# A delta-rule layer with a gated MoE layer behind it: which engine issues which DMA, and what the scheduler reckons

## The chip, the cores and the metric

The kernel runs on one core of a Trainium2 chip. Five engines of a core run their own instruction streams in order: TensorE (PE, with its weight loads as PEld), VectorE (DVE), ScalarE (ACT), GpSimd (POOL) and SyncE (SP), which here only issues DMAs. The metric is the device time in microseconds of one execution; the median of three runs of the kernel before is 515.21 us (514.75 to 515.44).

## The reference

Two layers follow each other. The first is a delta rule over 768 tokens, for 4 batches of 8 heads of 48 dimensions:

```python
k_n = k / (np.linalg.norm(k, axis=-1, keepdims=True) + 1e-06)
for t in range(S):
    kt, vt, bt = (k_n[:, :, t], v[:, :, t], beta[:, :, t, None])
    y[:, :, t] = np.einsum('bhd,bhde->bhe', q[:, :, t], state)
    v_old = np.einsum('bhde,bhd->bhe', state, kt)
    state = state + bt[:, :, :, None] * np.einsum('bhd,bhe->bhde', kt, vt - v_old)
```

Its output, as 3072 rows of 384, goes through an MLP with a softmax gate and a layer norm:

```python
h = x @ w_in                                    # 384 -> 1024
e = np.exp(h - np.max(h, axis=-1, keepdims=True))
solu = h * (e / (np.sum(e, axis=-1, keepdims=True) + 1e-09))
mu, var = np.mean(solu, -1), np.var(solu, -1)   # per row
out = ((solu - mu) / np.sqrt(var + 1e-06) * g_ln) @ w_out
```

## The kernel before, in words

The 768 tokens are cut into 12 chunks of 64. A unit is one chunk of two of the four batches, so there are 24 units of 128 rows (two batches of 64 tokens on the partitions), named chunk_half: 6_1 is chunk 6, second pair. Within a chunk the recurrence becomes matrix algebra with the inverse of a triangular matrix, and these inverses are made for several units at once: group m = 0 holds the two units of chunk 0, groups 1 to 5 four units each, group 6 the two units of chunk 11. (The prediction calls such a group a batch.)

A unit and its group pass these stages:

- **load and gram** (`load_kq`, `load_kv`, `gram`): keys and queries are loaded (tile kq; kv holds keys and values). TensorE forms k k^T and k q^T in PSUM; ScalarE copies the first to g, VectorE masks the second into pm. Two DMAs a unit store g into the DRAM tile gd (line 526).
- **inversion of a group** (`to_inv`, `norms`, `inv_begin`, `inv_step`, `inv_end`): gd is loaded back in another order as ginv (four or eight DMAs), VectorE makes norms and scales it to y, and GpSimd eliminates in 30 steps of two instructions (tiles itmp and y). `inv_end` copies y transposed on ScalarE, stores both to DRAM (zd, xd) and loads them in ten smaller DMAs in matmul order as zt, gx and gy. These DMAs that change an order are called relayouts; each moves runs of 128 bytes.
- **tlevel**: TensorE joins the 32-wide blocks into 64-wide inverses (mps, ScalarE's msb and zt).
- **chain**, the recurrence: kps and yps from the state, r = v - kps on VectorE, ups = inverse times r, ScalarE's copy u, then cps and yps, and the state's sum. The output is split into two fp16 parts xh (ScalarE) and xl (VectorE), which two DMA transposes turn into xth and xtl (`sp.transpose`, line 703).
- **moe_h**: 18 matmuls into h, then max, exponential e, product pr, the fp16 parts ph (ScalarE) and pl (VectorE), two DMA transposes to pth and ptl (line 745), a second pass e over pr, and statistics.
- **moe_out**: 24 matmuls into ops, oc on VectorE and ScalarE, and one DMA that stores the result (line 772).

All of it is not emitted as it is written. Every call is recorded as an operation with an engine, an occupancy and a latency in ns, and a priority that counts in units; `Recorder.order` (line 178) then plays the engines forward, and gives each engine, when it is free, the ready operation of the lowest priority number. It also follows which tiles of each ring are free. What it decides is emitted as a fixed order on each engine; on the chip an engine executes that order and waits where something is late. The occupancies come from `Engine` (a base and so much an element) and `Queue` (5 ns a KB, landing 2000 ns later). All 385 DMAs here stand on `sp`, SyncE's queue; a second `Queue` on ScalarE, `aq`, is made but not used. Each DMA signals one of eight semaphores in turn, so it also waits until the DMA eight before it, whichever queue that is on, has landed.

Of the kernel before, what the change touches and what calls it, by code (L numbers as in the profile page):

```python
# [16 lines left out]
P = 128  # L17
# [93 lines left out]


class Op:
    __slots__ = ("eng", "occ", "lat", "calls", "prio", "seq", "preds", "left", "succs", "avail", "start", "end", "roots", "slack")


class Recorder:
# [13 lines left out]

        return Pool()

    def add(self, eng, fn, args, kw, occ, lat, slack=0):
        views = [("out" if i == 0 else "in", a) for i, a in enumerate(args)]
        views += [("out" if k in ("out", "accum_out") else "in", a) for k, a in kw.items()]
        views = [(k, a) for k, a in views if isinstance(a, View)]
        if self.group is not None and self.group.calls and self.group.eng == eng:
            op = self.group
        else:  # L140
            op = Op()
            op.eng, op.occ, op.lat, op.calls, op.prio, op.seq = eng, 0.0, 0.0, [], self.prio, len(self.ops)
            op.preds, op.slack = {}, slack
# [34 lines left out]
    def order(self, free):  # L178
# [19 lines left out]
        while True:  # L198
            best = None
            for name, (t, fut, ready) in engs.items():  # L200
                if ready:
                    s = t
                elif fut:
                    s = max(t, fut[0][0])
                else:
                    continue
                if best is None or s < best[0]:
                    best = (s, name)
            if best is None:
                break  # L210
            t, name = best
            e = engs[name]
            while e[1] and e[1][0][0] <= t:
                o = heapq.heappop(e[1])[2]
                heapq.heappush(e[2], (o.prio, o.seq, o))
            o = heapq.heappop(e[2])[2]
            new = [r for r in o.roots if r.ring is not None and r.tile is None]
            wait = None
            for r in new:
                n = sum(x.ring is r.ring for x in new)  # L220
                f = sorted(r.ring.free)
                if len(f) < n:
                    wait = r.ring.waiting
                elif f[n - 1] > t and wait is None:
                    wait = f[n - 1]
            if isinstance(wait, list):
                wait.append(o)
                continue
            if wait is not None:
                heapq.heappush(e[1], (wait, o.seq, o))  # L230
                continue
            for r in new:
                r.tile = 0
                r.ring.free.remove(max(x for x in r.ring.free if x <= t))
            o.start = t
            e[0] = t + o.occ
            o.end = t + o.lat
            done.append(o)
            for r in o.roots:
                r.left -= 1  # L240
                r.free_at = max(r.free_at, t + o.occ if r.engs == {"DVE"} or r.engs == {"POOL"} else o.end)
                if not r.left and r.ring is not None:
                    r.ring.free.append(r.free_at)
                    for w in r.ring.waiting:
                        heapq.heappush(engs[w.eng][1], (max(w.avail, r.free_at), w.seq, w))
                    r.ring.waiting.clear()
            for s in o.succs:
                s.avail = max(s.avail, o.end if s.eng != name or name == "SP" else t + o.occ)
                s.left -= 1
                if not s.left:  # L250
                    s.avail += s.slack
                    heapq.heappush(engs[s.eng][1], (s.avail, s.seq, s))
# [15 lines left out]
class Engine:  # L268


    def __init__(self, rec, name, real, base, per, lat):
        self.rec, self.name, self.engine, self.base, self.per, self.lat = rec, name, real, base, per, lat

    def __getattr__(self, op):
        fn = getattr(self.engine, op)

        def call(*args, n=None, ns=None, slack=0, **kw):
            if ns is None:
                if n is None:
                    v = kw["in_"] if op == "tensor_reduce" else kw["out"] if "out" in kw else args[0]  # L280
                    n = v.count()
                ns = self.base + self.per * n + (190 if "accum_out" in kw else 0)
            return self.rec.add(self.name, fn, args, kw, ns, self.lat, slack)

        return call

# [1 line left out]
class Queue:  # L288


    def __init__(self, rec, name, real):
        self.rec, self.name, self.engine = rec, name, real

    def dma_start(self, kb, **kw):
        return self.rec.add(self.name, self.engine.dma_start, (), kw, kb * 5.0, 2000)

    def transpose(self, kb, **kw):
        return self.rec.add(self.name, self.engine.dma_start_transpose, (), kw, kb * 5.0, 2000)


def chunks_of(m):
# [4 lines left out]
def kernel(  # L306
# [23 lines left out]
    ps_ch, ps_y, ps_f, ps_h, ps_m = (pool(f"ps_{t}", n, **ps) for t, n in (("ch", 2), ("y", 1), ("f", 2), ("h", 1), ("m", 1)))  # L330

    real = nc
    pe = Engine(rec, "PE", nc.tensor, 0, 0, 200)
    dve = Engine(rec, "DVE", nc.vector, 150, 1.04, 80)
    act = Engine(rec, "ACT", nc.scalar, 110, 0.96, 100)
    gps = Engine(rec, "POOL", nc.gpsimd, 200, 1.8, 100)
    sp = Queue(rec, "SP", nc.sync)
    aq = Queue(rec, "ACT", nc.scalar)

    def half(b2):  # L340
        return slice(C * b2, C * b2 + C)
# [35 lines left out]
    def to_f32(u, raw, scale, n, nm):  # L377
# [10 lines left out]
        dve.tensor_scalar(out=u, in0=hi, scalar1=3, scalar2=0x3FFFFFF8, op0=ALU.logical_shift_left, op1=ALU.bitwise_and)  # L388
        dve.scalar_tensor_tensor(out=u, in0=lo, scalar=29, in1=u, op0=ALU.logical_shift_right, op1=ALU.bitwise_or)
        dve.scalar_tensor_tensor(out=u, in0=hi, scalar=-(1 << 30), in1=u, op0=ALU.bitwise_and, op1=ALU.bitwise_or)  # L390
        gps.tensor_tensor(out=f, in0=f, in1=c, op=ALU.mult)

    def load_w_in(k, q, t0, t1):
# [104 lines left out]
    def gram(m, u, t0):  # L498
# [30 lines left out]
    ginv, yt = {}, {}  # L529
# [31 lines left out]
    def inv_step(m, j):  # L561
# [3 lines left out]
        for eng, c0, c1 in parts:  # L565
            if c1 <= c0:
                continue
            c = c1 - c0
            tmp = p1.tile([P, 256], F32, tag=f"itmp{eng.name}", name=f"itmp_{m}_{j}_{c0}")
            tv = tmp[:, 0 : c * n].rearrange("p (c i) -> p c i", i=n)  # L570
            eng.tensor_tensor(
                out=tv, in0=y[:, c0:c1, j : j + 1].to_broadcast([P, c, n]),
                in1=b[:, j : j + 1, j + 1 : 32].to_broadcast([P, c, n]), op=ALU.mult,
            )
            eng.tensor_tensor(out=y[:, c0:c1, j + 1 : 32], in0=y[:, c0:c1, j + 1 : 32], in1=tv, op=ALU.add)

    def inv_end(m):
        y, x1 = yt[m], ginv[m]
# [12 lines left out]
        for b in range(4):  # L591
            blk = b % 2
            r0 = 32 * b
            rows = slice(r0, r0 + 32)
            sp.dma_start(kb=128, out=zz[rows, 0:n, blk * 32 : blk * 32 + 32], in_=zd[r0 : r0 + n].rearrange("l j i -> j l i"))
            if blk == 0:
                for t, r1 in ((xx, r0), (xy, r0 + 32)):
                    sp.dma_start(kb=128, out=t[r1 : r1 + 32, 0:n], in_=xd[r0 : r0 + n].rearrange("l j i -> j l i"))
            else:
                sp.dma_start(kb=128, out=xx[rows, 0:n], in_=src[rows, 0:n, 0:32])  # L600
        ztx[m], gxt[m] = zz, (xx, xy)


# [45 lines left out]
    def chain(m, u, tb, tu, tk):  # L649
# [59 lines left out]
    def moe_h(ch, bp, t0):  # L709
# [31 lines left out]
        dve.scalar_tensor_tensor(out=pl, in0=pr, scalar=sc, in1=ph, op0=ALU.mult, op1=ALU.subtract)  # L741
# [17 lines left out]
    def moe_out(ch, bp, t0):  # L759
# [169 lines left out]
```

## Time and profile before

| what | value |
|---|---|
| median of 3 runs | 515.21 us (514.75 to 515.44) |
| the profiled execution's own time | 512.04 us |
| its span, first to last instruction | 510.2 us |
| busy PE, DVE, POOL, ACT | 72%, 62%, 58%, 38% of the span |
| mean granted TensorE clock | 0.920 |
| DMA queue q1, share of 16 engines | 70.8%, 180560 packets, 71.06 MB |

The page gives each engine's busy time, the chain that ended last, and groups of instructions with the idle time before them and what ended it. Almost every row has line 265, the helper's line that emits; so instructions are told apart by their tiles (zt<-zd is a load of zt from zd). SPq is SyncE's queue: its rows are the time that one issue took, not the transfer. The first 100 us prepare the weights and the first two groups; from then on units follow each other.

### The profile page before, as it was taken

To read this page: it belongs to the slowest core of one execution; us is meant where nothing else is said; L and a number is where in the kernel's file an instruction comes from. 1 tells how busy PE (TensorE), PEld (TensorE's weight loads), DVE (VectorE), ACT (ScalarE), POOL (GpSimd) and SP (SyncE) were. 2 spreads that over 40 slices of the span, in tenths; PEclk is the share of its full clock that TensorE was granted. 3 is DMA by queue.
4 is the path that set the end of the run, shared out by engine and by line. 5 is a ranking of instruction groups with operands and counts; after the bars stand their busy time and mean duration, and the time that the engine had idled before them with its cause. 6 is when DMAs were issued, how large, how long until landed. Compare 5 with 4: busy or idle time off the path is not lost.

```text
span 510.2 us, 18246 instructions
## 1 busy us (share of the span) xinstructions
PE 368.2 (72%) x7744; PEld 233.9 (46%) x7744; DVE 318.6 (62%) x791; ACT 192.9 (38%) x382; POOL 294.0 (58%) x506
## 2 busy tenths in 40 slices
PE   3510070689579488997598997787969797899974
PEld 3410070455346345665366564444635464566532
DVE  3599999887884383655088664256597355455670
ACT  2210241465522143536144544224345345454450
POOL 3378385966558998984016886008989898100000
PEclk9999999877876699998799998898989899999998
DMA  8685662987989949977999587985656866744332
GB/s 212 159 255 98 155 169 65 161 171 174 172 162 165 179 113 160 168 135 161 189 165 144 145 162 151 160 162 95 107 118 144 145 114 128 131 64 99 73 68 61
DMA packets 180640, 72.21 MB, mean 142 GB/s; under 512 B 165520, under 2 KB 168976, under 8 KB 180560
## 3 DMA queue, kind: packets, MB, share of 16 engines
q1 hardware_dynamic: 180560, 71.06, 70.8%
q8 instruction: 60, 0.98, 0.9%
q14 instruction: 20, 0.16, 0.1%
HBM read 37.21 MB, written 16.52 MB: 105 GB/s over the span
## 4 chain that ended last, share of the span: by engine, by line
POOL 28%; PE 22%; DVE 19%; issue 10%; DMA 9%; SPq 7%; ACT 4%; POOLq 0%; DVEq 0%; ACTq 0%
POOL y L265 13%; POOL itmp L265 11%; PE h L265 7%; SPq L265 7%; PE ops L265 7%; DVE y L265 5%; DVE itmp L265 4%; DMA zt<-zd 3%; DMA ginv<-gd 3%; PE mps L265 2%; DVE wf L265 2%; DVE rst L265 1%; DVE st L265 1%; PE kps L265 1%; PE yps L265 1%
## 5 line engine op out<-in xcount | busy, mean ns | idle before, releaser
L265 POOL TENSOR_TENSOR y<-y,itmp 128x84 f32<-128x84 f32 (+16 forms) x190 | 100.7, 530 | 14.6
L265 POOL TENSOR_TENSOR itmp<-y,ginv 128x84 f32<-128x84 f32 (+16 forms) x190 | 93.3, 491 | 14.0
L265 DVE TENSOR_REDUCE st<-h 128x1 f32<-128x1024 f32 x24 | 29.3, 1222 | 87.5 <-PE h L265 82.2
L265 PE MATMUL qk<-kq 48*64 48x64 f32 x768 | 40.4, 269 | 24.9 <-DVE pm L265 15.6
L265 PE MATMUL gram<-kq 48*64 48x64 f32 x768 | 43.2, 270 | 18.8 <-DMA kq<-kq_dram 11.5
L265 POOL TENSOR_TENSOR st<-st,nhalf 128x1 f32<-128x1 f32 x24 | 13.2, 551 | 64.1 <-DVE st L265 64.1
L265 PEld LDWEIGHTS gram<-kq 48*64 48x64 f32 x768 | 37.5, 178 | 25.7 <-ACT g L265 6.3
L265 PEld LDWEIGHTS <-pth 128*128 128x128 f16 x384 | 37.6, 99 | 25.5 <-issue 1.7
L265 PE MATMUL h<-win_hi,xtl 128*128 128x512 f16 x144 | 45.4, 419 | 5.3 <-DVE pr L265 2.6
L265 PE MATMUL mps<-zt,gx 32*32 32x32 f32 x768 | 13.5, 205 | 48.6 <-issue 28.9
L265 PE MATMUL h<-win_lo,xth 128*128 128x512 f16 x144 | 46.7, 421 | 1.7 <-POOL win_lo L265 1.7
L265 PEld LDWEIGHTS qk<-kq 48*64 48x64 f32 x768 | 35.8, 178 | 25.3 <-DVE pm L265 16.1
L265 PEld LDWEIGHTS <-xth 128*128 128x128 f16 x288 | 28.4, 105 | 39.7 <-issue 14.8
L265 PE MATMUL ops<-wout_hi,ptl 128*128 128x384 f16 x192 | 38.7, 345 | 8.7 <-DMA ptl<-pl 6.8
L265 PE MATMUL h<-win_hi,xth 128*128 128x512 f16 x144 | 43.4, 411 | 0.0
L265 ACT ACTIVATE e<-h,st 128x1024 f32<-128x1024 f32 x24 | 26.7, 1114 | 38.0 <-DVE st L265 26.4
L265 POOL TENSOR_SCALAR_AFFINE_SELECT y<-y 128x1024 f32<-128x1024 f32 x7 | 9.4, 1346 | 53.5 <-DVE y L265 53.5
L265 DVE TENSOR_SCALAR st<-st 128x1 f32<-128x1 f32 (+1 forms) x216 | 35.5, 165 | 5.6
L265 PE MATMUL ops<-wout_lo,pth 128*128 128x384 f16 x192 | 36.9, 334 | 0.0
L265 PEld LDWEIGHTS mps<-zt,gx 32*32 32x32 f32 x768 | 10.1, 117 | 56.9 <-issue 34.8
L265 PE MATMUL ops<-wout_hi,pth 128*128 128x384 f16 x192 | 35.5, 326 | 0.0
L265 PE MATMUL cps<-u,kv 64*64 64x48 f32 x704 | 28.9, 235 | 9.1 <-ACT u L265 3.2
(94 smaller groups left out, 860.4 us busy)
## 6 DMA issues: line engine op xcount, KB each, us to landing
kq<-kq_dram SPq DMA_DIRECT2D x48, 192.0 KB, 4.5
kv<-kv_dram SPq DMA_DIRECT2D x24, 384.0 KB, 4.3
gd<-g SPq DMA_DIRECT2D x48, 128.0 KB, 3.3
out_dram<-oc SPq DMA_DIRECT2D x24, 192.0 KB, 2.2
zd<-y SPq DMA_DIRECT2D x7, 512.0 KB, 2.6
wi<-w_in_dram SPq DMA_DIRECT2D x6, 512.0 KB, 4.4
wo<-w_out_dram SPq DMA_DIRECT2D x8, 384.0 KB, 4.0
ginv<-gd SPq DMA_DIRECT2D x20, 128.0 KB, 4.2
```

Source lines behind the costliest of these rows:

```text
L265: fn(*[real(a) for a in args], **{k: real(a) for k, a in kw.items()})
```

## The change

Three kinds of edit. **Issue:** the transposes (xth, xtl, pth, ptl), the stores of g and the stores of the result go to `aq`, ScalarE's queue; loads and relayouts stay on SyncE. **Reckoning:** a DMA on ScalarE occupies it for 400 ns in the scheduler; on SyncE it counts its KB, at least 500 ns, or 1.2 ns a run; a landing is 2300 ns later; TensorE's times are multiplied by 1.06; some VectorE operations get times of their own; the 190 ns for an accumulated output are dropped. **Holding:** `rec.hold(pm)` lets the plan take pm's buffer when the gram matmuls start.

```diff
             for s in o.succs:
-                s.avail = max(s.avail, o.end if s.eng != name or name == "SP" else t + o.occ)
+                s.avail = max(s.avail, o.end if s.eng != name or o.queued else t + o.occ)
...
-                ns = self.base + self.per * n + (190 if "accum_out" in kw else 0)
-            return self.rec.add(self.name, fn, args, kw, ns, self.lat, slack)
+                ns = self.base + self.per * n
+            return self.rec.add(self.name, fn, args, kw, ns * self.scale, self.lat, slack)
...
-    def dma_start(self, kb, **kw):
-        return self.rec.add(self.name, self.engine.dma_start, (), kw, kb * 5.0, 2000)
+    def __init__(self, rec, name, real, issue=None):
+        self.rec, self.name, self.engine, self.issue = rec, name, real, issue
+
+    def add(self, fn, kw, ns):
+        occ = ns if self.issue is None else self.issue
+        return self.rec.add(self.name, fn, (), kw, occ, 2300 + ns - occ, queued=True)
+
+    def dma_start(self, kb, runs=0, **kw):
+        return self.add(self.engine.dma_start, kw, max(500.0, kb * 5.0, runs * 1.2))
 
     def transpose(self, kb, **kw):
-        return self.rec.add(self.name, self.engine.dma_start_transpose, (), kw, kb * 5.0, 2000)
+        return self.add(self.engine.dma_start_transpose, kw, kb * 5.0)
...
-    pe = Engine(rec, "PE", nc.tensor, 0, 0, 200)
+    pe = Engine(rec, "PE", nc.tensor, 0, 0, 200, 1.06)
...
-    aq = Queue(rec, "ACT", nc.scalar)
+    aq = Queue(rec, "ACT", nc.scalar, 400)
...
+            rec.hold(pm)
...
-            sp.dma_start(kb=128, out=gdt[m][half(b2), u], in_=g[half(1 - b2)])
+            aq.dma_start(kb=128, out=gdt[m][half(b2), u], in_=g[half(1 - b2)])
...
-                    kb=128, out=gi[32 * b + 16 * z : 32 * b + 16 * z + n],
+                    kb=128, runs=32 * n, out=gi[32 * b + 16 * z : 32 * b + 16 * z + n],
...
-            sp.transpose(kb=96, out=t, in_=x)
+            aq.transpose(kb=96, out=t, in_=x)
...
-            sp.transpose(kb=256, out=t, in_=x)
+            aq.transpose(kb=256, out=t, in_=x)
...
-        sp.dma_start(kb=192, out=out[ch, bp], in_=t)
+        aq.dma_start(kb=192, out=out[ch, bp], in_=t)
```

The diff does not show what the scheduler makes of it. In the rows below a number behind a tile's name is a buffer's; zd_3, xd_3, zt_1 and gx_3 belong to group 3, and a pair such as 4_0 is a unit.

SyncE's queue around group 3's relayouts, before:

```order
L265 DMA xd_3_3316<-ginv_3_2308 32x1024 x2
L265 DMA zt_1_278<-zd_3_3296 32x32x32 x3
L265 DMA gx_3_2399<-xd_3_3316 32x32x32
L265 DMA gy_3_3421<-xd_3_3316 32x32x32
L265 DMA_TRANSPOSE xth_4_0_3431<-xh_4_0_3417 128x3x128
L265 DMA gx_3_2399<-xd_3_3316 32x32x32
L265 DMA gd_4_2357<-g_8_0_3436 64x512 x2
L265 DMA_TRANSPOSE pth_3_0_3464<-ph_3_0_3444 128x8x128
L265 DMA_TRANSPOSE xtl_4_0_3476<-xl_4_0_3459 128x3x128
L265 DMA_TRANSPOSE ptl_3_0_3491<-pl_3_0_3467 128x8x128
L265 DMA gy_3_3421<-xd_3_3316 32x32x32
L265 DMA zt_1_278<-zd_3_3296 32x32x32
```

and now:

```order
L265 DMA xd_3_3312<-ginv_3_2288 32x1024 x2
L265 DMA kq_9_0_3319<-kq_dram 48x1024 x2
L265 DMA zt_1_272<-zd_3_3286 32x32x32
L265 DMA gx_3_2472<-xd_3_3312 32x32x32
L265 DMA gy_3_3432<-xd_3_3312 32x32x32
L265 DMA zt_1_272<-zd_3_3286 32x32x32 x2
L265 DMA gx_3_2472<-xd_3_3312 32x32x32
L265 DMA gy_3_3432<-xd_3_3312 32x32x32
L265 DMA zt_1_272<-zd_3_3286 32x32x32
```

The four transposes and the two stores of g that stood between the relayouts are gone from this queue; a prefetch of kq stands ahead.

SyncE's queue between group 4's last relayout and the loads of ginv for group 5, before:

```order
L265 DMA zt_0_188<-zd_4_4686 32x32x32
L265 DMA gd_5_4100<-g_10_1_4730 64x512 x2
L265 DMA_TRANSPOSE xth_6_1_4853<-xh_6_1_4843 128x3x128
L265 DMA kq_11_1_4858<-kq_dram 48x1024 x2
L265 DMA_TRANSPOSE pth_5_1_4932<-ph_5_1_4862 128x8x128
L265 DMA_TRANSPOSE ptl_5_1_4956<-pl_5_1_4894 128x8x128
L265 DMA_TRANSPOSE xtl_6_1_4971<-xl_6_1_4885 128x3x128
L265 DMA out_0_dram<-oc_5_0_4936 128x384
L265 DMA ginv_5_5011<-gd_5_4100 32x32x32 x4
```

and now:

```order
L265 DMA gx_4_3721<-xd_4_4637 32x32x32
L265 DMA gy_4_4741<-xd_4_4637 32x32x32
L265 DMA zt_0_189<-zd_4_4609 32x32x32
L265 DMA ginv_5_4826<-gd_5_4135 32x32x32 x4
L265 DMA kq_11_1_4918<-kq_dram 48x1024 x2
```

The loads of ginv follow the relayouts directly; kq comes behind them.

ScalarE between the exponential of unit 5_1 and the copy u of unit 7_0, before:

```order
L265 ACTIVATE ph_5_1_4862<-pr_5_1_4845,st_5_1_4818 128x1024
L265 ACTIVATE msb_4_0_4892<-mps0_4_0_4866 128x128
L265 ACTIVATE e_5_1_4826,st_5_1_4818<-pr_5_1_4845,st_5_1_4818 128x1024
L265 ACTIVATE oc_5_0_4936<-oc_5_0_4936,st_5_0_4492 128x384
L265 COPY zt_0_188<-mps0_4_0_4866 32x4x32 x2
L265 COPY zt_0_188<-mps32_4_0_4940 32x4x32 x2
L265 ACTIVATE msb_4_1_5009<-mps0_4_1_4974 128x128
L265 COPY u_7_0_5014<-ups_7_0_4992 128x384
```

and now, from the transpose of xh on:

```order
L265 DMA_TRANSPOSE xth_6_1_4851<-xh_6_1_4844 128x3x128
L265 ACTIVATE ph_5_1_4875<-pr_5_1_4847,st_5_1_4822 128x1024
L265 ACTIVATE msb_4_0_4890<-mps0_4_0_4856 128x128
L265 DMA_TRANSPOSE pth_5_1_4895<-ph_5_1_4875 128x8x128
L265 ACTIVATE e_5_1_4829,st_5_1_4822<-pr_5_1_4847,st_5_1_4822 128x1024
L265 DMA_TRANSPOSE ptl_5_1_4957<-pl_5_1_4892 128x8x128
L265 DMA_TRANSPOSE xtl_6_1_4960<-xl_6_1_4883 128x3x128
L265 COPY zt_0_189<-mps0_4_0_4856 32x4x32 x2
L265 COPY zt_0_189<-mps32_4_0_4900 32x4x32 x2
L265 ACTIVATE oc_5_0_4955<-oc_5_0_4955,st_5_0_4501 128x384
L265 DMA out_0_dram<-oc_5_0_4955 128x384
L265 ACTIVATE msb_4_1_5019<-mps0_4_1_4978 128x128
```

ScalarE's own work keeps its order nearly; four transposes and a store now stand between its instructions. The copy u of unit 7_0 is the next row.

More of the change, by code (lines that the diff above doesn't have):

```diff
@@ L113 @@
 class Op:
-    __slots__ = ("eng", "occ", "lat", "calls", "prio", "seq", "preds", "left", "succs", "avail", "start", "end", "roots", "slack")
+    __slots__ = ("eng", "occ", "lat", "calls", "prio", "seq", "preds", "left", "succs", "avail", "start", "end", "roots", "slack", "queued")
 class Recorder:
@@ L132, in pool, with add @@
         return Pool()
-    def add(self, eng, fn, args, kw, occ, lat, slack=0):
+    def add(self, eng, fn, args, kw, occ, lat, slack=0, queued=False):
         views = [("out" if i == 0 else "in", a) for i, a in enumerate(args)]
@@ L142, in add @@
             op.eng, op.occ, op.lat, op.calls, op.prio, op.seq = eng, 0.0, 0.0, [], self.prio, len(self.ops)
-            op.preds, op.slack = {}, slack
+            op.preds, op.slack, op.queued = {}, slack, queued
             self.ops.append(op)
@@ L268, with __init__ @@
 class Engine:
-    def __init__(self, rec, name, real, base, per, lat):
-        self.rec, self.name, self.engine, self.base, self.per, self.lat = rec, name, real, base, per, lat
+    def __init__(self, rec, name, real, base, per, lat, scale=1.0):
+        self.rec, self.name, self.engine, self.base, self.per, self.lat, self.scale = rec, name, real, base, per, lat, scale
     def __getattr__(self, op):
@@ L281, in call @@
                     n = v.count()
-                ns = self.base + self.per * n + (190 if "accum_out" in kw else 0)
-            return self.rec.add(self.name, fn, args, kw, ns, self.lat, slack)
+                ns = self.base + self.per * n
+            return self.rec.add(self.name, fn, args, kw, ns * self.scale, self.lat, slack)
         return call
 class Queue:
-    def __init__(self, rec, name, real):
-        self.rec, self.name, self.engine = rec, name, real
-    def dma_start(self, kb, **kw):
-        return self.rec.add(self.name, self.engine.dma_start, (), kw, kb * 5.0, 2000)
+    def __init__(self, rec, name, real, issue=None):
[5 more added lines that the diff above has]
+        return self.add(self.engine.dma_start, kw, max(500.0, kb * 5.0, runs * 1.2))
     def transpose(self, kb, **kw):
-        return self.rec.add(self.name, self.engine.dma_start_transpose, (), kw, kb * 5.0, 2000)
+        return self.add(self.engine.dma_start_transpose, kw, kb * 5.0)
 def chunks_of(m):
@@ L387, in to_f32 @@
         u = u.bitcast(I32)
-        dve.tensor_scalar(out=u, in0=hi, scalar1=3, scalar2=0x3FFFFFF8, op0=ALU.logical_shift_left, op1=ALU.bitwise_and)
-        dve.scalar_tensor_tensor(out=u, in0=lo, scalar=29, in1=u, op0=ALU.logical_shift_right, op1=ALU.bitwise_or)
-        dve.scalar_tensor_tensor(out=u, in0=hi, scalar=-(1 << 30), in1=u, op0=ALU.bitwise_and, op1=ALU.bitwise_or)
+        dve.tensor_scalar(ns=250 + 1.3 * n, out=u, in0=hi, scalar1=3, scalar2=0x3FFFFFF8, op0=ALU.logical_shift_left, op1=ALU.bitwise_and)
+        dve.scalar_tensor_tensor(ns=250 + 1.3 * n, out=u, in0=lo, scalar=29, in1=u, op0=ALU.logical_shift_right, op1=ALU.bitwise_or)
+        dve.scalar_tensor_tensor(ns=250 + 1.3 * n, out=u, in0=hi, scalar=-(1 << 30), in1=u, op0=ALU.bitwise_and, op1=ALU.bitwise_or)
         gps.tensor_tensor(out=f, in0=f, in1=c, op=ALU.mult)
@@ L570, in inv_step @@
             tv = tmp[:, 0 : c * n].rearrange("p (c i) -> p c i", i=n)
+            ns = 230 + 1.04 * c * n if eng is dve else None
             eng.tensor_tensor(
-                out=tv, in0=y[:, c0:c1, j : j + 1].to_broadcast([P, c, n]),
+                ns=ns, out=tv, in0=y[:, c0:c1, j : j + 1].to_broadcast([P, c, n]),
                 in1=b[:, j : j + 1, j + 1 : 32].to_broadcast([P, c, n]), op=ALU.mult,
             )
-            eng.tensor_tensor(out=y[:, c0:c1, j + 1 : 32], in0=y[:, c0:c1, j + 1 : 32], in1=tv, op=ALU.add)
+            eng.tensor_tensor(ns=ns, out=y[:, c0:c1, j + 1 : 32], in0=y[:, c0:c1, j + 1 : 32], in1=tv, op=ALU.add)
     def inv_end(m):
@@ L594, in inv_end @@
             rows = slice(r0, r0 + 32)
-            sp.dma_start(kb=128, out=zz[rows, 0:n, blk * 32 : blk * 32 + 32], in_=zd[r0 : r0 + n].rearrange("l j i -> j l i"))
+            sp.dma_start(kb=128, runs=1024, out=zz[rows, 0:n, blk * 32 : blk * 32 + 32], in_=zd[r0 : r0 + n].rearrange("l j i -> j l i"))
             if blk == 0:
                 for t, r1 in ((xx, r0), (xy, r0 + 32)):
-                    sp.dma_start(kb=128, out=t[r1 : r1 + 32, 0:n], in_=xd[r0 : r0 + n].rearrange("l j i -> j l i"))
+                    sp.dma_start(kb=128, runs=1024, out=t[r1 : r1 + 32, 0:n], in_=xd[r0 : r0 + n].rearrange("l j i -> j l i"))
             else:
-                sp.dma_start(kb=128, out=xx[rows, 0:n], in_=src[rows, 0:n, 0:32])
+                sp.dma_start(kb=128, runs=1024, out=xx[rows, 0:n], in_=src[rows, 0:n, 0:32])
         ztx[m], gxt[m] = zz, (xx, xy)
@@ L740, in moe_h @@
         act.activation(ph, pr, AF.Copy, scale=sc)
-        dve.scalar_tensor_tensor(out=pl, in0=pr, scalar=sc, in1=ph, op0=ALU.mult, op1=ALU.subtract)
+        dve.scalar_tensor_tensor(ns=1420, out=pl, in0=pr, scalar=sc, in1=ph, op0=ALU.mult, op1=ALU.subtract)
         pts = []
```

## The prediction

> **What bounds the kernel now.** I read the page first, then the busy time by stage, then what TensorE and SyncE wait for, then SyncE's queue around those waits.
>
> ```profile
> PE 368.2 (72%) x7744; PEld 233.9 (46%) x7744; DVE 318.6 (62%) x791; ACT 192.9 (38%) x382; POOL 294.0 (58%) x506
> POOL 28%; PE 22%; DVE 19%; issue 10%; DMA 9%; SPq 7%; ACT 4%; POOLq 0%; DVEq 0%; ACTq 0%
> ```
>
> No engine is full over the whole span, and the chain that ended last changes engine all the time; SyncE's queue (SPq) and transfers (DMA) hold 16% of it. So the stages have to be taken apart. The columns of the next view are busy us of PE, PEld, DVE, ACT and POOL, then the granted clock, the busy share of the DMA engines and GB/s.
>
> ```profile
> 100.00:205.00 105.00, 80.48 (x1744) 50.35 (x1743) 70.34 (x157) 40.27 (x84) 79.76 (x117) 0.78 0.88 161
> 205.00:485.00 280.00, 241.95 (x5093) 149.98 (x5091) 159.59 (x415) 122.52 (x246) 151.25 (x274) 0.95 0.71 135
> ```
>
> From 205 us on TensorE works 241.95 of 280 us. That stage is TensorE's, with 280 - 241.95 = 38.05 us of gaps, and only what closes or opens such gaps can move the end. The gaps that a transfer ends are these (the wait is in brackets, first the group's total in 205 to 485 us):
>
> ```profile
> PE mps L265 <- DMA zt<-zd: 14.0, 4, 5.4
> 250.75 0.64 PE L265 MATMUL mps<-zt,gx 32*32 32x32 f32 x30 [5.44 <-DMA zt<-zd]
> 324.67 0.45 PE L265 MATMUL mps<-zt,gx 32*32 32x32 f32 x30 [3.37 <-DMA zt<-zd]
> 345.04 0.22 PE L265 MATMUL mps<-msb,gy 32*32 32x32 f32 x2 [2.62 <-DVE pm L265]
> 447.16 0.45 PE L265 MATMUL mps<-zt,gx 32*32 32x32 f32 x30 [2.40 <-DMA zt<-zd]
> ```
>
> Three are the first matmuls that read a batch's relaid inverse zt (batches 3, 4 and 6); the row at 345.04 waits for VectorE, which is late with batch 5's norms.
>
> **What the change takes off SyncE.** In the same 280 us SyncE issued these, 18 units of each transpose (columns: count, then min/median/max ns of one issue):
>
> ```profile
> L265 SPq DMA_DIRECT2D out_dram<-oc x19: 342/382/1722, 204.7 to 480.6; - x19
> L265 SPq DMA_TRANSPOSE ptl<-pl x18: 1232/1282/2154, 210.9 to 479.3; - x18
> L265 SPq DMA_TRANSPOSE pth<-ph x18: 1231/1260/2602, 212.2 to 477.5; - x18
> L265 SPq DMA_TRANSPOSE xtl<-xl x18: 1180/1218/1804, 214.9 to 475.2; - x18
> L265 SPq DMA_TRANSPOSE xth<-xh x18: 1178/1210/2564, 216.2 to 473.9; - x18
> L265 SPq DMA_DIRECT2D gd<-g x16: 450/588/1760, 240.9 to 354.1; - x16
> ```
>
> At the medians that is 18 x (1.282 + 1.260 + 1.218 + 1.210) = 89.5 us, 16 x 0.588 = 9.4 us and 19 x 0.382 = 7.3 us, together 106.2 us of issue, which leave SyncE and come to stand on ScalarE.
>
> **Term 1, the relayouts (gain 7.84 us).** This is SyncE's queue within batch 3's burst:
>
> ```profile
> 239.01 1.21 SPq L265 DMA_TRANSPOSE xth<-xh  x1
> 240.27 0.58 SPq L265 DMA_DIRECT2D gx<-xd  x1
> 240.89 1.21 SPq L265 DMA_DIRECT2D gd<-g  x2
> 242.20 1.33 SPq L265 DMA_TRANSPOSE pth<-ph  x1
> 243.63 1.36 SPq L265 DMA_TRANSPOSE xtl<-xl  x1
> 245.08 1.26 SPq L265 DMA_TRANSPOSE ptl<-pl  x1
> 246.39 0.57 SPq L265 DMA_DIRECT2D gy<-xd  x1
> 247.03 0.60 SPq L265 DMA_DIRECT2D zt<-zd  x1
> ```
>
> Between the burst's own rows stand 1.21 + 1.21 + 1.33 + 1.36 + 1.26 = 6.37 us of other issues, and the last zt is the one that TensorE waits 5.44 us for. In the changed order nothing stands between them. Batch 6 has the same picture:
>
> ```profile
> 436.31 2.54 SPq L265 DMA_TRANSPOSE xth<-xh  x1
> ...
> 440.64 1.23 SPq L265 DMA_TRANSPOSE pth<-ph  x1
> 441.97 1.39 SPq L265 DMA_TRANSPOSE ptl<-pl  x1
> 443.41 1.27 SPq L265 DMA_TRANSPOSE xtl<-xl  x1
> 444.73 0.57 SPq L265 DMA_DIRECT2D zt<-zd  x1
> ```
>
> 6.43 us of others against a wait of 2.40 us. Batch 4's burst has none in it, so its 3.37 us stays. I take both waits whole, 5.44 + 2.40 = 7.84 us; the other end is 0, if the transfers and not their issue time the landing (a rival below).
>
> **Term 2, batch 5's inverse (gain 2.62 us).** Before its four ginv loads SyncE is busy without a break:
>
> ```profile
> 321.31 1.40 SPq L265 DMA_DIRECT2D gd<-g  x2
> 322.81 1.24 SPq L265 DMA_TRANSPOSE xth<-xh  x1
> ...
> 330.12 1.72 SPq L265 DMA_DIRECT2D out_dram<-oc  x1
> 331.90 2.63 SPq L265 DMA_DIRECT2D ginv<-gd  x4
> ```
>
> VectorE then does the norms late, and TensorE waits the 2.62 us above. In the changed order the ginv loads follow batch 4's relayouts at once, held only by the landing of the last gd, so up to 331.90 - 322.81 = 9.1 us earlier. I take the 2.62 us whole; the other end is 0, since VectorE must still do the same work in order.
>
> **Term 3, ScalarE (loss 2 us).** It gains 106.2 us of issue to its 122.52 us of work: 228.7 of 280 us, 12.7 us a unit of 280 / 18 = 15.6 us. So it does not run out of time, but it is near. The scheduler reckons 107 issues at 0.4 us, 42.8 us, so 63.4 us, 3.5 us a unit, are not in its plan: ScalarE will be late by that where a unit's four transposes stand in a row. Who waits then? The tightest link is the copy u, between ups and cps on TensorE:
>
> ```profile
> 456.26 1.06 PE ups L265 x32
> 457.32 3.13 PE h L265 x14
> 457.37 0.48 ACT L265 COPY u<-ups 128x384 f32<-128x384 f32 x1 [1.24 <-PE ups L265]
> ```
>
> Its cover is 3.13 - 0.48 = 2.65 us of h matmuls, and in that row ScalarE stood idle 1.24 us before it. A lateness of 3.5 us exceeds 2.65 us by 0.85 us. The trace has no DMA issue on ScalarE, so the bounds are 0 (all hidden) and 0.85 x 18 = 15.3 us (every unit); I take 2 us, some two or three units, because with 15.6 - 12.7 = 2.9 us to spare a unit the lateness does not add up. It can fall below nothing only if the transposes land sooner; no gap in that stage rests on that, so I give it none.
>
> The Trainium skill (Perfetto Trace Analysis, Sequencer Loop) says that a sequencer pushes an engine's instruction into a queue and executes control instructions itself; by that an issue could run beside the activation ahead of it, and the term would be near its end of 0. No run here shows it yet.
>
> **Startup and end (0).** From 100 to 205 us ScalarE is busy 40.27 of 105 us and gets some 4 transposes and two stores ahead of batch 2's last gram, which delays its inversion; the changed order puts unit 2's h and another ops ahead of that batch's matmuls, which fills the time. Bounds: 5 us more (4 x 1.24 us), 2 us less. At the end the last ptl stands behind two ScalarE instructions, not beside them: 0 to 1.28 us, one issue.
>
> **Other edits.** The reckoned costs remove no instruction; they only set the order. The hold on pm makes the gram matmuls wait for a free pm in the plan, which VectorE waits for anyway: 0, and without that cover one gram group.
>
> **The sum.** The profiled execution took 512.04 us (span 510.2). 512.04 - 7.84 - 2.62 + 2 = 503.6 us. The median of the runs, 515.21, lies 3.17 us above it, so I forecast 507 us.
>
> **Rivals.**
>
> ScalarE sets the pace (slower). An in-order engine holds all its copies behind an issue that waits for its source or for a landing eight transfers back. From 2.9 us of such waits a unit on, ScalarE's loop is longer than TensorE's. If it waits out one median landing a unit, 4.3 us for ptl, it is 1.4 us over, 1.4 x 18 = 25.2 us, less the gains of 10.5: 512.04 + 14.7 = 526.7, as a median 530. For it: in 205 to 485 us SyncE waited ahead of its issues, most of all for ScalarE, and a transfer takes long to land (the second row is its us from issue):
>
> ```profile
> SPq L265 <- ACT e L265: 19.2, 7, 6.2
> ptl<-pl SPq DMA_TRANSPOSE x24, 4.3
> DMA to landing us min/median/max: 1.9/3.7/7.0
> ```
>
> Against it: a wait of an issue for ScalarE's own result costs next to nothing on ScalarE, whose order it is already in.
>
> The DMA engines time the landing (no gain). The share column speaks for it in batch 3, not in batch 6:
>
> ```profile
> 240.00:250.00 10.00, 5.30 (x173) 3.85 (x171) 1.86 (x3) 1.58 (x3) 0.52 (x2) 0.89 1.05 161
> 440.00:450.00 10.00, 7.60 (x186) 4.55 (x181) 2.31 (x7) 1.35 (x4) 1.44 (x4) 1.00 0.62 111
> ```
>
> Then the 5.44 us stay, term 2's load lands no sooner either, and the sum is 512.04 - 2.40 + 2 = 511.6, as a median 515. The Trainium skill says the same as a rule (DMA: Bandwidth & Descriptors, Issuing engines are not separate DMA queues): all queues share the 16 engines, and a second issuing engine saves only issue time, usually small beside the transfer. The trace agrees with the first half at 1.05, not with "small": 1.2 us of issue against 4 us to landing.
>
> The order fits better everywhere (more gain). The new costs are nearer to the rows (a transfer lands after 3.7 us in the median, as the last row above has it, where 2.0 was reckoned), so half of the remaining 38.05 - 10.5 = 27.6 us of gaps may close: 503.6 - 13.8 = 489.8, as a median 493.
>
> **Chances.** Forecast 0.40 (its own range 503 to 513: term 3 at 0 with 2 us less at startup, 503.6 - 2 - 2 + 3.2, or term 3 at 8 us, half its bound, 503.6 + 6 + 3.2), better order 0.20, ScalarE sets the pace 0.27, DMA engines 0.13. About 0.2% (1 us) is what can be told from no change. Faster: 0.40 + 0.20 + 0.05 of the last = 0.65; within 0.2%: 0.08; slower: 0.27. The range reaches from 490 to 528, which leaves out the far halves of the two outer cases.
>
> **What would show it.** Right: no transpose row on SPq between relayouts, the zt waits of batches 3 and 6 under 1 us each, TensorE's gaps in the middle stage near 28 us, ScalarE's queue at about 1.2 us an issue. Wrong: TensorE waiting for u, zt or e of ScalarE by more than 10 us in all, or zt waits that stay with a DMA share near 1.

## The result, and the profile after

The changed kernel takes 579.1 us (575.35 to 583.14, four runs) against 515.04 of the kernel before: a ratio of 1.1245 [1.1168, 1.1321], 64 us slower. 507 us was forecast, and 490 to 528 given as the range. A ratio, here and below, leaves out runs in a slower state; of the changed kernels only defer had such runs, two of its four.

The page of the changed kernel (span 577.8 us, mean granted clock 0.864, where it was 0.920), and the page's DMA queues, show that the move took place: 28% of the DMA engines' time now belongs to ScalarE's queue, q10.

```profile
PE 391.3 (68%) x7744; PEld 248.4 (43%) x7744; DVE 316.3 (55%) x791; ACT 195.9 (34%) x382; POOL 290.2 (50%) x506
q1 hardware_dynamic: 102608, 42.73, 36.3%
q10 hardware_dynamic: 77952, 28.33, 27.9%
```

TensorE has the same 7744 matmuls and is busy 23 us longer. To see where the time lies I cut each kernel at two landmarks that all have, the starts of the 8th and of the 20th first activation e<-h of a unit: startup, twelve units of the middle, rest. First before, then after:

```profile
257.79 1.11 ACT L265 ACTIVATE e<-h,st 128x1024 f32<-128x1024 f32 x1 [6.07 <-DVE st L265]
449.92 1.11 ACT L265 ACTIVATE e<-h,st 128x1024 f32<-128x1024 f32 x1 [1.98 <-PE mps L265]
```

```profile
283.94 1.11 ACT L265 ACTIVATE e<-h,st 128x1024 f32<-128x1024 f32 x1 [5.94 <-DVE st L265]
508.87 1.11 ACT L265 ACTIVATE e<-h,st 128x1024 f32<-128x1024 f32 x1 [2.73 <-PE mps L265]
```

Startup is 26.1 us longer, the middle 32.8 (192.1 to 224.9), the rest 8.6 (60.3 to 68.9). The busy times of that middle, in the columns that the prediction explained, before and after:

```profile
257.80:449.90 192.10, 163.66 (x3577) 101.34 (x3576) 113.03 (x294) 83.12 (x168) 122.02 (x219) 0.95 0.72 137
```

```profile
283.90:508.90 225.00, 181.91 (x3578) 112.41 (x3577) 111.22 (x296) 84.99 (x169) 117.00 (x218) 0.85 0.66 114
```

Busy time times clock is 163.66 x 0.95 = 155.5 and 181.91 x 0.85 = 154.6 us: nearly the same work. So 18.3 of the 32.9 us are longer busy time at a lower clock and 43.1 - 28.4 = 14.7 us are more idle time. This splits the time of one execution; it does not say what a full clock would win back. What TensorE waits for in that middle, first two rows of before, then after:

```profile
PE qk L265 <- ACT zt L265: 0.2, 1, 0.2
PE ups L265 <- DVE r L265: 0.7, 2, 0.5
```

```profile
PE qk L265 <- ACT zt L265: 14.1, 4, 5.3
PE ups L265 <- DVE r L265: 12.3, 5, 3.2
PE mps L265 <- ACT msb L265: 4.8, 2, 3.1
```

One of the stalls, in TensorE's row and then in ScalarE's timeline (ACTq rows are issues):

```profile
311.94 0.36 PE L265 MATMUL qk<-kq 48*64 48x64 f32 x1 [5.30 <-ACT zt L265]
```

```profile
306.03 1.29 ACTq L265 DMA_TRANSPOSE pth<-ph  x1
307.37 1.15 ACT L265 ACTIVATE e<-pr,st 128x1024 f32<-128x1024 f32 x1 [1.37 <-issue]
307.48 1.21 ACTq L265 DMA_TRANSPOSE xtl<-xl  x1
308.42 0.19 ACT L265 ACTIVATION_READ_ACCUMULATOR e<-pr,st 128x1 f32 x1
308.78 2.55 ACTq L265 DMA_TRANSPOSE ptl<-pl  x1
311.37 0.52 ACT L265 COPY zt<-mps 32x128 f32<-32x128 f32 x2 [2.76 <-issue]
```

The copies zt, which empty the PSUM tile that qk needs, stand behind the issues of xtl and ptl (1.21 + 2.55 us), and e stands behind that of pth. VectorE waits in its own order for ph and e ahead of r, and so r is late for ups. In the middle it waits 32.6 us for them (1.3 before), over the whole run 67.6 us:

```profile
DVE st L265 <- ACT e L265: 27.6, 18, 7.7
DVE pl L265 <- ACT ph L265: 25.5, 17, 4.9
DVE pr L265 <- ACT e L265: 14.5, 12, 5.9
```

And this is the clock in windows of 4 us around that stall (the third number from the end):

```profile
304.00:308.00 4.00, 2.64 (x73) 1.57 (x71) 2.45 (x4) 2.29 (x4) 3.53 (x7) 1.00 0.36 79
308.00:312.00 4.00, 0.06 (x4) 0.06 (x4) 0.68 (x2) 1.21 (x5) 3.61 (x8) 0.51 1.25 117
312.00:316.00 4.00, 4.00 (x126) 3.91 (x126) 0.69 (x1) 1.33 (x3) 3.53 (x7) 0.50 0.65 145
316.00:320.00 4.00, 4.00 (x29) 1.61 (x19) 0.00 (x0) 0.52 (x2) 3.54 (x6) 0.71 0.23 51
320.00:324.00 4.00, 4.00 (x112) 2.65 (x111) 2.93 (x9) 1.58 (x3) 3.59 (x6) 1.00 0.23 53
```

After a stall of 5.3 us TensorE is full, at half clock for 4 us and at 0.71 for the next 4: 4 x 0.5 + 4 x 0.29 = 3.2 us of TensorE's work not done on top of the stall. The middle has seven stalls of 3 us or more after the change (27.2 us, the first at 293.13, the last at 456.56) and three before (11.2 us, at 324.67, 378.64 and 433.84). The Trainium skill (TensorE: Matmul & The Clock Gate, Part 1: The HAM clock gate) states this as a rule: half clock after an idle window of about 3.4 us, full clock after about as long a busy one. The rows of this stall agree in the main, though the clock is at half (0.51 from 308 to 312 us) soon after the stall begins at 306.64. Other stretches do not: in the same middle the clock is also 0.50 from 396.8 to 400.2 us and in three more stretches behind stalls of only 1.7 to 2.4 us, and in the kernel before it stays at 1.00 behind the 3.1 us stall that ends at 433.84.

Nor does a lower clock go with as much time from run to run. Of the 44 runs of the kernel before that stand beside the experiments, 43 took 511.0 to 516.1 us at mean clocks from 0.887 to 0.933, and the four runs of defer2 (below) took 552.7, 558.1, 559.0 and 559.2 us at 0.883, 0.914, 0.871 and 0.868. So a lower mean clock need not cost its share of the time: TensorE may only come later to the same wait. What a stall costs beyond its own length is not shown.

### The profile page after: what moved, and what is told of

Read it like the earlier page. It is cut to its first block, busy times and chain, and to the rows that moved or that the text cites. A ratio compares the mean times of both kernels' runs of the same rounds, so it can differ in the third digit from the quotient of the medians.

```text
span 577.8 us, 18184 instructions
## 1 busy us (share of the span) xinstructions
PE 391.3 (68%) x7744; PEld 248.4 (43%) x7744; DVE 316.3 (55%) x791; ACT 195.9 (34%) x382; POOL 290.2 (50%) x506
## 5 line engine op out<-in xcount | busy, mean ns | idle before, releaser
L265 POOL TENSOR_TENSOR y<-y,itmp 128x84 f32<-128x84 f32 (+16 forms) x190 | 96.9, 510 | 19.9 <-ACT y L265 5.8
L265 POOL TENSOR_TENSOR itmp<-y,ginv 128x84 f32<-128x84 f32 (+16 forms) x190 | 93.2, 491 | 14.1
L265 PE MATMUL gram<-kq 48*64 48x64 f32 x768 | 45.9, 277 | 43.9 <-ACT g L265 20.7
L265 PEld LDWEIGHTS gram<-kq 48*64 48x64 f32 x768 | 39.3, 184 | 52.1 <-ACT g L265 22.9
L265 PE MATMUL qk<-kq 48*64 48x64 f32 x768 | 42.1, 278 | 21.6 <-ACT zt L265 14.3
L265 PE MATMUL ups<-r,zt 64*64 64x48 f32 x704 | 34.1, 261 | 32.0 <-DVE r L265 29.0
L265 DVE TENSOR_SCALAR st<-st 128x1 f32<-128x1 f32 (+1 forms) x216 | 35.8, 166 | 33.6 <-ACT e L265 27.6
L265 PE MATMUL h<-win_hi,xtl 128*128 128x512 f16 x144 | 50.7, 451 | 3.7 <-DMA xtl<-xl 2.8
L265 PEld LDWEIGHTS ups<-r,zt 64*64 64x64 f32 x704 | 31.2, 177 | 39.0 <-DVE r L265 30.2
L265 DVE SCALAR_TENSOR_TENSOR pl<-pr,st,ph 128x1024 f16<-128x1024 f32 x24 | 32.9, 1373 | 25.7 <-ACT ph L265 25.5
L265 PE MATMUL h<-win_hi,xth 128*128 128x512 f16 x144 | 45.7, 427 | 0.0
L265 POOL TENSOR_TENSOR kv<-kv,nrt 128x384 f32<-128x384 f32 x22 | 19.5, 897 | 44.7 <-DMA kv<-kv_dram 21.9
L265 ACT ACTIVATE e<-pr,st 128x1024 f32<-128x1024 f32 x24 | 27.5, 1148 | 41.9 <-DVE pl L265 14.5
```

What stands on the lines that cost most here:

```text
L265: fn(*[real(a) for a in args], **{k: real(a) for k, a in kw.items()})
```

## The experiments

All ran beside runs of the kernel before (514.3 to 514.7 us in each group). The table has each kernel's landmarks in its profiled execution, worked out as above; the kernels are explained below it.

| kernel | median us | ratio [95%] | start of 8th e | 8th to 20th e | clock |
|---|---|---|---|---|---|
| before | 515.2 | 1 | 257.8 | 192.1 | 0.920 |
| changed | 579.1 | 1.125 [1.117, 1.132] | 283.9 | 224.9 | 0.864 |
| a_sp | 527.5 | 1.026 [1.023, 1.029] | 265.6 | 197.6 | 0.909 |
| b_act | 530.8 | 1.034 [1.028, 1.039] | 264.8 | 202.6 | 0.905 |
| reck | 531.4 | 1.032 [1.029, 1.035] | 265.8 | 199.2 | 0.924 |
| true | 549.2 | 1.067 [1.062, 1.072] | 281.3 | 198.8 | 0.920 |
| o_stores | 537.9 | 1.045 [1.041, 1.050] | 274.4 | 196.1 | 0.907 |
| o_transp | 563.2 | 1.094 [1.087, 1.100] | 267.2 | 222.9 | 0.872 |
| defer | 570.0 | 1.097 [1.090, 1.104] | | | |
| defer2 | 558.5 | 1.084 [1.079, 1.089] | 287.2 | 201.4 | 0.914 |
| hold | 519.5 | 1.010 [1.006, 1.013] | 262.6 | 191.9 | 0.924 |
| cost | 527.8 | 1.025 [1.023, 1.027] | 260.4 | 203.5 | 0.924 |
| land | 516.3 | 1.003 [1.000, 1.005] | 241.9 | 207.1 | 0.912 |
| runs | 528.6 | 1.027 [1.022, 1.033] | 268.7 | 193.1 | 0.925 |
| dvens | 524.0 | 1.018 [1.014, 1.022] | 267.4 | 192.5 | 0.879 |
| b_out | 517.4 | 1.006 [1.004, 1.008] | 260.0 | 192.6 | 0.917 |
| b_own | 577.1 | 1.124 [1.120, 1.128] | 276.7 | 224.8 | 0.873 |
| honest | 536.4 | 1.044 [1.039, 1.049] | 275.0 | 194.9 | 0.920 |

Defer's landmarks are left out, since its profiled execution was the slowest of its four (574.6 us); by its ratio it stands at 1.0973 x 514.3 = 564 us. The split by landmarks is safe between kernels of one order (changed, a_sp, o_stores, o_transp). Where the order differs, work can move across a landmark: land's eighth e starts 15.9 us earlier than before and its middle is 15.0 us longer, at almost the same time.

### The queue and the order apart: a_sp, b_act, reck, true

The order of the change, issued from SyncE:

```diff
-    aq = Queue(rec, "ACT", nc.scalar, 400)
+    aq = Queue(rec, "ACT", nc.sync, 400)
```

> Changed order as it is (planned as if ScalarE issued at 400 ns each), but the transposes, the stores of g and of the result are issued from SyncE's queue at the same places of the plan. Theory 1 (the issues block ScalarE, VectorE and then TensorE queue behind it): 500 to 525 us, and VectorE's waits for ScalarE's e and ph fall from about 78 us to under 20. Theory 2 (the changed order itself is bad, whoever issues): 560 to 580 us.

The order before, with the stores of G, the transposes and the stores of the result through this queue:

```diff
-    aq = Queue(rec, "ACT", nc.scalar)
+    aq = Queue(rec, "SP", nc.scalar)
```

> The kernel before with its own order, only that the same DMAs are issued from ScalarE's queue at the places of the old plan. Theory 1 (issues block ScalarE): 555 to 590 us. Theory 2 (the order): 510 to 530 us.

All of the new reckoning, every DMA planned for SyncE and issued from it:

```diff
-    aq = Queue(rec, "ACT", nc.scalar, 400)
+    aq = Queue(rec, "SP", nc.sync)
```

> All reckoned times, runs and the hold of the change, but every DMA planned on and issued from SyncE. Theory 1: 495 to 520 us. Theory 2 (the reckoning made the order bad): 540 to 580 us.

The changed kernel, with the issues reckoned at about what they take (`cost` is what an issue occupies of ScalarE):

```diff
-        occ = ns if self.issue is None else self.issue
+        occ = ns if self.issue is None else cost
...
+        return self.add(self.engine.dma_start, kw, max(500.0, kb * 5.0, runs * 1.2), 540)
...
+        return self.add(self.engine.dma_start_transpose, kw, kb * 5.0, 1300)
```

> The change with ScalarE's issue reckoned at what the trace shows, 1300 ns a transpose and 540 ns a plain DMA instead of 400 ns each. If the loss comes from a plan that does not know the blocking: 510 to 535 us. If ScalarE's queue is simply too full of issues: 560 to 580 us.

Neither theory stands alone. The order costs 12.9 us (a_sp), the queue in the old order 16.1 (b_act), and the two together 64: 35 us belong to the combination, an order packed with 400 ns issues that take 1200. In a_sp VectorE's waits for e and ph fall from 67.6 us (about 78 in the expectation) to 11.9, as theory 1 said, and yet the time misses its range by 2.5 us. The true reckoning gives back 30 us, by the landmarks in the middle, which falls from 224.9 to 198.8 us; its startup stays late (281.3).

### Stores or transposes: o_stores, o_transp

Both keep the change's order row for row; a second queue, reckoned alike, issues one kind from SyncE.

```diff
+    asp = Queue(rec, "ACT", nc.sync, 400)
...
-            t = p2.tile([P, 8, P], F16, tag=f"pt{s}", name=f"pt{s}_{nm}")
-            aq.transpose(kb=256, out=t, in_=x)
+            asp.transpose(kb=256, out=t, in_=x)
```

> The order of the change, row for row, but the 96 transposes are issued from SyncE; only the stores of G and of the result go from ScalarE. Theory of two places (the stores delay the startup, the transposes the units in the middle): with everything on SyncE the eighth e came at 265.6 us and with everything on ScalarE at 283.9, and twelve units in the middle took 197.6 and 224.9; so this one keeps most of the late start (+18) and loses the long middle (-27) and some of the tail: about 545 to 555 us. Rival, that only the sum of both fills ScalarE (each alone is hidden): 525 to 535. Rival, that only the stores matter: 570 to 580.

> The counterpart: the order of the change, the stores of G and of the result issued from SyncE, the 96 transposes from ScalarE. Theory of two places: startup as with everything on SyncE, the middle as in the changed kernel: 555 to 565 us, and VectorE again waits some 60 us for ScalarE's e and ph. Rival, that only the sum of both fills ScalarE: 525 to 535. Rival, that only the stores matter: 525 to 530.

Against a_sp the stores cost 10.4 us and the transposes 35.7, together 46.1 of the 51.6 us by which the change is above a_sp; so it is not only their sum that is too much. With the order's 12.9 us that accounts for 59.0 of the 64 us. The middles of the two:

```profile
274.40:470.50 196.10, 165.18 (x3577) 101.88 (x3576) 110.22 (x294) 83.21 (x168) 117.25 (x218) 0.93 0.72 131
```

```profile
267.20:490.10 222.90, 181.64 (x3577) 111.64 (x3576) 111.82 (x296) 84.41 (x168) 117.10 (x218) 0.85 0.63 116
```

The transposes make the whole loss of the middle, lower clock included, and nearly none of the startup (267.2 against a_sp's 265.6); the stores the reverse (274.4). The two waits of TensorE come with the transposes: in o_transp's middle qk waits 14.0 us for zt and ups 12.1 us for r, in a_sp's 0.2 and 4.7. The o_stores time fell below its expected 545 to 555: the startup's 18 us need both, since the stores alone cost 8.8 there and the transposes alone 1.6.

How a store is late at startup, in the changed kernel's ScalarE rows:

```profile
20.68 0.59 ACT L265 COPY g<-gram 128x512 f32<-128x512 f32 x1 [6.88 <-DMA gd<-g]
25.12 1.73 ACTq L265 DMA_DIRECT2D gd<-g  x2
26.90 0.66 ACT L265 ACTIVATE wc_i<-wi 128x512 f32<-128x512 f32 x1 [5.63 <-DMA ginv<-gd]
62.51 1.93 ACT L265 COPY ginv<-y 128x1024 f32<-128x1024 f32 x1 [22.89 <-DVE y L265]
95.56 4.82 ACTq L265 DMA_TRANSPOSE xth<-xh  x1
100.50 1.97 ACT L265 COPY ginv<-y 128x1024 f32<-128x1024 f32 x1 [4.97 <-DVE wf L265]
```

In a_sp the same three copies, the third of G and those of the first two inverses, stand at:

```profile
15.82 0.59 ACT L265 COPY g<-gram 128x512 f32<-128x512 f32 x1 [2.83 <-PE qk L265]
55.94 1.93 ACT L265 COPY ginv<-y 128x1024 f32<-128x1024 f32 x1 [18.72 <-DVE y L265]
89.43 2.02 ACT L265 COPY ginv<-y 128x1024 f32<-128x1024 f32 x1 [0.43 <-DVE y L265]
```

ScalarE's third copy waits 6.88 us until an earlier store has landed, and the store at 25.12 was held until a load of ginv on the other queue had landed (the row behind it names that load): the eight semaphores are common to both queues. The inverse is then copied 6.6 us later, and the next one 11.1 us later, with an issue of xth in front of it that took 4.82 us. Why that issue took so long when most take 1.2 is open, and so is what adds the rest up to the 18 us of the eighth e.

### Copies behind issues: defer, defer2

The order of the change is left as planned, and then a transpose on ScalarE is emitted behind the computing instruction next to it if that is a copy of zt (defer), or behind such copies, copies u and an activation e (defer2), as long as nothing between reads it.

```diff
-        emit(done)
+        emit(behind(done))
```

> The changed kernel, its order kept, but on ScalarE a transpose whose next computing instruction is a copy of zt is issued behind that copy instead of ahead of it. In the middle of the changed kernel TensorE stalls three times for 3.8 to 5.3 us on qk, which waits for a copy of zt that stands behind the issues of xtl and ptl, and after a stall of 3 us or more its clock stays at half for some microseconds. Theory (copies behind issues): these stalls go, 14 us, and some 9 us of half clock with them: 555 to 565. Rival (ScalarE's issue time itself is the bound, whatever the place): 574 to 584.

> As in the run before, and the issues also pass the copies u and the activations e, so that e no longer stands behind pth. VectorE waits 67.6 us for e and ph in the changed kernel, and r, which TensorE's ups waits for, is behind these waits. Theory (copies behind issues): the twelve units in the middle fall from 225 us to 198 to 205 us, and the time to 547 to 560. Rival (issue time is the bound): 570 or more. If it isn't better than the run before, e wasn't in TensorE's way.

Defer's runs spread from 560.7 to 574.6 us, all below the changed kernel's lowest; it gains 9 us by their median and 15 by the ratio, at the edge of its 555 to 565 or outside. In its profiled execution qk still waits 9.3 us for zt in the middle, so the stalls that it was to end are fewer but not gone. Defer2 gains 20.6 us; its middle, 201.4 us, and its time, 558.5, lie within what was expected, with the same number of issues on ScalarE. So for these 20.6 us the issue time as such is not the bound; its place is. The other 44 us above the kernel before stay. TensorE's two waits in the middle of defer2 are:

```profile
PE qk L265 <- ACT zt L265: 1.6, 3, 0.7
PE ups L265 <- DVE r L265: 5.5, 3, 2.4
```

VectorE's longest wait for ScalarE after the change, st for e (27.6 us), is nearly gone, while that for ph stays at 19.9; and in this execution the clock of the middle is back at 0.93:

```profile
DVE st L265 <- ACT e L265: 2.9, 2, 2.3
```

```profile
287.20:488.60 201.40, 168.48 (x3578) 103.11 (x3577) 111.29 (x295) 82.95 (x169) 118.17 (x218) 0.93 0.75 129
```

### The order alone: hold, cost, land, runs, dvens

Hold is the kernel before with the one added line `rec.hold(pm)`; cost is reck without that line and without the 1.06 on TensorE. The other three change one of the costs in the kernel before: land the landing (`2000` to `2300`), runs the transfers' occupation (`max(500.0, kb * 5.0, runs * 1.2)`), dvens VectorE's durations.

> The kernel before with one line of the change: the group of gram and qk also takes its place in pm's buffers (rec.hold(pm)), nothing else. All of the new reckoning together, with every DMA on SyncE, cost 16.8 us (531.4). If the hold makes the order worse, since gram and qk can't run ahead any more: 522 to 532. If the costs do: 512 to 518.

> The kernel with all of the new reckoning and everything on SyncE (531.4 us), without the hold on pm and without the 1.06 on TensorE: the transfers' new costs and landings and VectorE's new durations are left. If these make the order worse: 525 to 535. If it was the hold or the 1.06: 512 to 518.

> The kernel before with one number of the reckoning changed: a transfer lands 2300 ns after its issue and not 2000. Theory A (one of the new costs is bad): two of the three runs with one cost each stay within 512 to 517 and the third is at 524 to 530. Theory B (the order before is a good one among many, and any other order costs some): all three between 516 and 526, with no one of them giving the whole 13 us. This one by A: 512 to 517.

> The kernel before with only the transfers' new occupation of SyncE: at least 500 ns, and 1.2 ns a run, so 1230 ns and not 640 for a relayout (the trace has 0.3 to 0.6 us for such an issue, so this cost is too high). By theory A this is the bad one, since it makes SyncE look full: 524 to 530. By theory B: 516 to 526.

> The kernel before with only the new durations of VectorE's instructions (and without the 190 ns of an accumulation). They are nearer to the trace (pl takes 1.37 us, reckoned now 1.42 and before 1.21). By theory A: 512 to 517. By theory B: 516 to 526.

The hold costs 4.7 us, the landing 1.6, the durations 9.3 and the transfers' occupation 13.9, as much as all the costs together (13.0). Neither theory holds: more than one term costs, land's 0.3% is hardly more than nothing, and they don't add. In runs and dvens the middle is as short as before (193.1 and 192.5 us), and the loss lies in the startup; in cost it lies in the middle (203.5). Dvens' numbers are nearer to the trace than the ones they replace, so a truer cost did not make a better order here. What differs in these orders was not followed further.

### Parts of the move: b_out, b_own, honest

In the order before, only the 24 stores of the result go from ScalarE (b_out); with them also xth and pth, whose sources ScalarE wrote (b_own):

```diff
-            sp.transpose(kb=256, out=t, in_=x)
+            (aq if s == "h" else sp).transpose(kb=256, out=t, in_=x)
```

> The kernel before, order and all, with only the 24 stores of the result issued from ScalarE. Each follows its own activation, takes 0.34 us, and SyncE no longer waits for it. If what costs is the 1.2 us of a transpose and waiting for others: 512 to 516, faster or the same. If any issue on ScalarE costs: 518 or more.

> The kernel before, order and all, with the stores of the result and the transposes xth and pth, whose sources ScalarE wrote itself, issued from ScalarE; xtl and ptl, whose sources VectorE wrote, stay on SyncE, and G's stores too. All of them on ScalarE cost 16.1 us. If the waits for VectorE's results are what costs: 512 to 518. If the issue time costs: half of the 16 us, 520 to 525.

Even b_out is 3 us slower (2 to 4), between its two expectations. B_own contradicts both of its theories: half of the transposes on ScalarE cost 63 us where all of them cost 16. The likely reason is in what SyncE's queue waits for:

```profile
SPq L265 <- DMA pth<-ph: 108.5, 21, 11.8
SPq L265 <- DMA xth<-xh: 60.6, 12, 10.4
```

Of the waits of SyncE's queue, 33 with 169 us in all end with the landing of a transpose of ScalarE's queue; nearly all of them stand ahead of a transpose of SyncE's own, with prefetches and relayouts behind it. That they make up the 63 us is argued; no run has the two queues without these waits. The Trainium skill (DMA: Bandwidth & Descriptors, Silent corruption: two transposing streams in flight at once) says that two queues' transposes can corrupt each other and must wait for each other's completion. The trace shows the waits; what they prevent no run here shows. The change itself has all transposes on one queue and doesn't pay this.

Honest is the move planned with measured issue times (1300 and 540 ns), with the hold, and all other costs as before:

> The move alone: the change's queues, planned with 1300 ns a transpose and 540 ns a store on ScalarE, with the hold on pm, and otherwise the old costs (landing 2000, no 1.06, VectorE and transfers as before). With the new costs this was 549.2 us. Theory: the move costs by itself (startup behind ScalarE's queue), and the old costs take back 13 us: 530 to 538. Rival (the prediction's terms 1 and 2, the move gains once its cost is planned): 505 to 515.

536.4 us is as the theory expected, 22 us behind the kernel before. By the landmarks its middle is 194.9 us, so with the right issue times and the old costs the move costs almost nothing there (2.8 us), but also gains nothing; the startup is 17 us late. TensorE's waits of its whole run:

```profile
PE gram L265 <- ACT g L265: 16.9, 6, 5.7
PE mps L265 <- ACT msb L265: 11.3, 6, 3.7
PE mps L265 <- DMA zt<-zd: 6.7, 2, 4.9
```

## Why the prediction was wrong

**What bounds, terms 1 and 2 (gain 10.46 us).** The mechanism was right, but no gain shows. No issue of a transpose stands between relayouts any more, and TensorE's waits for zt<-zd fall from 18.0 us to 1.3 in the changed kernel and 6.7 in honest. But the time did not follow: in honest g and msb of ScalarE are waited for in their place (5.4 and 1.2 us before), and the middle is 2.8 us longer. The rival that the DMA engines time the landing is not what happened.

**Term 3 (loss 2 us, bounds 0 to 15.3) is the step that failed.** The transposes alone measured 25 us in the twelve units of the middle (o_transp against a_sp), some 2 us a unit, and 36 with the rest. Two of its points hold: an issue takes 1.2 us on ScalarE as on SyncE (columns: count, then min/median/max ns), and ScalarE did not run out of time (85.0 us of work and 84.6 of issues in the 225 us of the middle).

```profile
L265 ACTq DMA_TRANSPOSE xth<-xh x24: 1194/1226/4818, 95.6 to 540.1; - x24
L265 ACTq DMA_TRANSPOSE ptl<-pl x24: 1247/1286/3817, 133.0 to 564.5; - x24
```

What failed is "the tightest link is the copy u". The step looked for ScalarE's results that TensorE waits for directly and took one; the results that matter were zt, which gives a PSUM tile back, and e and ph, which only VectorE waits for, with r behind them. TensorE waited for u 1.1 us in the middle, for qk's zt 14.1 and for ups' r 12.3. So the bound, 0.85 us a unit behind the cover of u, was laid on the wrong link: the stalls that came were up to 5.3 us long. Defer2 takes 20.6 us back by moving issues behind such results. A lower clock came with the stalls, and the prediction has no term for it; how much time it took stays open.

By the rule cited there (the Trainium skill, Perfetto Trace Analysis, Sequencer Loop) the term would be near 0. The trace agrees with the mechanism, and not with that end:

```profile
290.04 1.15 ACT L265 ACTIVATE e<-pr,st 128x1024 f32<-128x1024 f32 x1 [1.36 <-DVE pl L265]
290.14 1.20 ACTq L265 DMA_TRANSPOSE xtl<-xl  x1
```

The issue runs beside the activation ahead of it. But two issues in a row, or one whose source is the instruction ahead, hold what stands behind.

**Startup and end (0, bounds -2 to 5, and 0 to 1.28).** Wrong by 26 us and 8.6 us. Of the 26 us, 7.8 come with the order alone (a_sp). The step counted four transposes and two stores ahead of one gram; it did not follow the stores of the first two groups, whose copies wait for the stores' own landings and, through the eight common semaphores, for SyncE's loads. The end's loss comes with the transposes: from the 20th e on o_transp takes 70.2 us, a_sp 61.4.

**Other edits ("they only set the order", 0).** Wrong by 13 to 17 us with no DMA moved (a_sp, cost, reck). An edit that only sets the order was taken for one without a cost; a single cost term moved the time by 1.6 to 14 us, always upwards.

**Rivals and chances.** The rival that ScalarE sets the pace had the direction, at 530 and 0.27; its mechanism, issues that hold the copies behind them, is the one seen, but it was priced by one landing a unit, where the rows show issues ahead of zt (1.21 + 2.55 us), and it had no part for the order's 12.9 us. "Order fits better" (0.20) fell: no run with the new costs was faster than before. The sign to look for, waits for u, zt or e over 10 us, came true: 14.3 and 13.9 us for zt alone over the whole run.

```profile
PE qk L265 <- ACT zt L265: 14.3, 5, 5.3
PE gram L265 <- ACT zt L265: 13.9, 3, 12.0
```

No kernel tried beats the one before.

## What to carry to other kernels

On a queue whose engine computes nothing a DMA issue holds only other issues; on an engine that computes it holds every later instruction of that engine, so before moving it list all results that come behind it and follow each to its waiters on every engine, and the buffers it gives back. A busy time at a lower clock is no price by itself: compare runs of one kernel at different clocks first. Where a planner sets the order, take an edit of its costs as a new order, here 0.3 to 3.2% slower, and not as nothing; and plan a moved issue with its measured time.

## What the runs showed of the hardware

TensorE's granted clock tends to be lower where it stalls: 0.85 in middles with seven stalls of 3 us or more (changed, o_transp), 0.93 to 0.95 in those with one to three (before, a_sp, o_stores, true). But this count does not set it. Defer's middle has three such stalls and 0.85, dvens' three and 0.90, and b_act's three, less idle time than before (27.1 against 28.4 us) and 0.89. In b_act the clock stays at 0.50 for 10.2 us in which TensorE is never idle, behind a stall of 1.1 us; why is open:

```profile
286.10:296.30 10.20, 10.20 (x145) 5.91 (x143) 2.75 (x5) 2.64 (x6) 9.18 (x16) 0.50 0.60 137
```

Transposes issued from two queues wait for each other's landing, up to 11.8 us at a time (b_own). And an issue of a transpose, 1.2 us in the median, can take 4.8 us; four kernels with stores and transposes on ScalarE (changed, true, defer, defer2) showed it at the same xth (4.62 to 4.82 us), while two others (honest, b_act) issued it there in 1.35 and 1.60.
